# The second tile's normalisation on Pool, and the first transposes copied in another order

## The chip, the cores and the metric

The kernel runs on one core of a Trainium2 chip. The metric is the device time of one execution in microseconds (us). Its engines are TensorE (PE in the profile, with its weight loads as PEld), VectorE (DVE), ScalarE (ACT), Pool (GpSimd) and SyncE (SP), which here only issues transfers. Each engine runs its own instructions in their written order and waits on semaphores for the others.

## The reference

A layer norm without weights feeds two branches, and both are added to x: sliding-window attention (16 heads of 28, window 256) and a gated FFN.

```python
def reference(A_x, A_wqkv, A_wo, B_x, B_w_gate, B_w_up, B_w_down):   # S 2048, D 448, F 1792, bf16
    x = A_x
    xn = (x - mean(x)) / sqrt(var(x) + 1e-5)
    q, k, v = (xn @ A_wqkv) split into 16 heads of 28
    scores = q k^T * 28**-0.5, kept where 0 <= i - j < 256
    attn = softmax(scores) v, heads joined, @ A_wo
    ffn = (gelu(xn @ B_w_gate) * (xn @ B_w_up)) @ B_w_down
    return x + attn + ffn
```

## The kernel before

The 2048 rows of x are 16 tiles of 128 rows (t = 0 to 15), and four blocks of 512 rows (qb = 0 to 3). The body is scheduled by hand: the order in which the instructions are written is the order in which each engine gets them, and semaphores that the framework adds hold an engine until what it reads is there.

Each block needs the normalised x transposed: `xnT` holds the 448 features on partitions, in chunks of 128, and the rows along the free dimension. For one tile of the first block this is made in steps:

- `stat(t)` (L155, L156) on VectorE: the mean and variance of each row.
- `rstd(t, n)` (L160, L161) on ScalarE: Ln and Exp, which give one over the standard deviation.
- `norm(t)` (L170) on VectorE: subtract the mean, multiply by that, 448 elements on each of 128 partitions, into a tile `xn` in bf16. Four buffers of `xn` exist.
- `transp(t, copy, tag)` (L185, L186): four transposes on TensorE into a PSUM bank, and a copy of 512 elements a partition out of it into `xnT`. The bank is given by the tag, "b2" or "b3", and each tag has one buffer; so the transposes of tile 2 wait for the copy of tile 0, and those of tile 3 for the copy of tile 1.

The later tiles are transposed by DMA (`dma_transp`, L176). Behind the first four tiles TensorE does the V products of tiles 0 and 1 (`v_dense`, L190), then the q and k products of the first head group over all four tiles (`proj`, L190). They need all of `xnT` of the first block. From then on, scores (L684), their exponentials on ScalarE (L688), the products with V (L656) and the FFN (L488, L394) are interleaved by the lists in `plan`.

`warmup(n)` (L150) is n matmuls on zeroes ahead of the first data. `pads` (L743) copies weights of q and k into their padded layout. On Pool stand, before all this, the making of the identity and memsets of `v_sb`; the next work on it is the move of half a chunk of `xnT` (L770), behind all four copies, and then the masks (L117).

The order at the start of the first block, as written:

```python
    norm(0)
    stat(2)
    rstd(2, 1)
    transp(0, nc.scalar.copy, "b2")
    norm(1)
    stat(3)
    rstd(3, 1)
    warmup(1)
    transp(1, nc.scalar.copy, "b3")
```

Of the kernel before, what the change touches and what calls it, by code (L numbers as in the profile page):

```python
# [27 lines left out]
def kernel(  # L28
# [11 lines left out]
    nc = tc.nc  # L40
# [22 lines left out]
    x_sb = const.tile([P, NT, D], bf16, name="x_sb")  # L63
# [79 lines left out]
    mv_all = const.tile([P, NT, 2], f32, name="mv_all")  # L143
# [3 lines left out]
    def warmup(n):  # L147
        wps = phase[0].pool.tile([P, 2, QB], f32, name="wps", tag="s")
        for i in range(n):
            nc.tensor.matmul(wps[:, i % 2, :], lhsT=warm[:, 0:P], rhs=warm[:, 0:QB], start=True, stop=True)  # L150


    def stat(t):
        st = work.tile([P, nc.vector.BN_STATS_DIM], f32, name="st")
        nc.vector.bn_stats(out=st[:, :], in_=x_sb[:, t, :])  # L155
        nc.vector.bn_aggr(out=mv_all[:, t, :], in_=st[:, :])  # L156

    def rstd(t, n):
        lnv = work.tile([P, 4], f32, name="lnv")
        nc.scalar.activation(out=lnv[:, 0:n], in_=mv_all[:, t:t + n, 1], func=ACT.Ln, bias=eps_t[:, 0:1], scale=1.0)  # L160
        nc.scalar.activation(out=rstd_all[:, t:t + n], in_=lnv[:, 0:n], func=ACT.Exp, scale=-0.5)  # L161

    xns = {}

    def norm(t):
        xn = work.tile([P, 4, P], bf16, name="xn", bufs=4)
        xf = xn[:, :, :].rearrange("p a b -> p (a b)")
        both = ((0, D, 0), (D, 64, 384))
        for lo, n, src in both if t > 3 else both[:1]:
            nc.vector.tensor_scalar(out=xf[:, lo:lo + n], in0=x_sb[:, t, src:src + n], scalar1=mv_all[:, t, 0:1],  # L170
                                    scalar2=rstd_all[:, t:t + 1], op0=ALU.subtract, op1=ALU.mult)
        xns[t] = xn

# [4 lines left out]
    def transp(t, copy, tag):  # L178


        tp = psum.tile([P, 8, P], bf16, name="tp", tag=tag, bufs=1)
        xn = xns.pop(t)
        xf = xn[:, :, :].rearrange("p a b -> p (a b)")
        for c, lo in enumerate((0, P, 2 * P, D - P)):
            nc.tensor.transpose(out=tp[:, c, :], in_=xf[:, lo:lo + P], identity=ident[:, :])  # L185
        copy(out=xnT[:, :, t * P:(t + 1) * P], in_=tp[:, 0:4, :])  # L186
# [16 lines left out]
    def take(name, cols=QB, tag=None):  # L203

        tag = tag or spare[0]
        spare.remove(tag)
        ps = psum.tile([P, QB], f32, name=name, tag=tag, bufs=1)[:, 0:cols]  # L210
        held[id(ps)] = tag, ps
        return ps
# [6 lines left out]
    def v_dense(t, pv):  # L219
        mm3(pv, lambda c: xnT[:, c, t * P:(t + 1) * P], lambda c: wv[:, c, :], True, False)  # L220
# [531 lines left out]
    stat(1)  # L752
    rstd(1, 1)
    norm(0)
    stat(2)
    rstd(2, 1)
    transp(0, nc.scalar.copy, "b2")
    norm(1)
    stat(3)
    rstd(3, 1)  # L760
    warmup(1)
    transp(1, nc.scalar.copy, "b3")
    pvs = [take("pv", D)]
    v_dense(0, pvs[0])
    norm(2)
    transp(2, nc.scalar.copy, "b2")
    norm(3)
    pads(nc.vector.tensor_copy, wqp, slice(0, 1))
# [290 lines left out]
```

## Time and profile before

| what | us |
|---|---|
| median of 3 runs | 212.53 (212.52 to 212.82) |
| the profiled execution's own time | 212.69 |
| its span in the profile | 210.8 |
| TensorE busy | 205.1 (97% of the span) |
| VectorE busy | 157.8 (75%) |
| ScalarE busy | 132.0 (63%) |
| Pool busy | 48.4 (23%) |

In the profile's rows, the first number is the start in us from the span's start, the second the duration; then engine, line, operation, what it writes and reads, shape and count. A bracket holds the time that the engine stood idle before, and what ended it. Successive instructions on an engine overlap a little: the next one starts some hundredths to a tenth of a us before the row of the one ahead ends. The ends of TensorE's rows are modelled.

### The profile page before, as it was taken

The page shows a single profiled execution, that of the slowest core. Times are in us where ns is not written, and L with a number is a line of the kernel's source. Part 1 is how long each engine was busy: PE and PEld are TensorE (multiplying, and loading weights), DVE is VectorE, ACT ScalarE, POOL GpSimd, SP SyncE. Part 2 cuts the span into 40 slices and gives each one's busy share as a digit, 9 for nine tenths or more (in the row PEclk, how much of TensorE's full clock was granted, in tenths as well). Part 3 has the DMA queues.
Part 4 walks back from the last instruction along what each step waited for, and adds up shares of the span by engine and source line. Part 5 has one row for each costly group of instructions (what it writes and reads, how often), then busy time and mean ns, then how long its engine had stood idle before and what let it go on. Part 6 is the DMA issues. An engine that isn't in the chain of part 4 may idle for free.

```text
span 210.8 us, 6335 instructions
## 1 busy us (share of the span) xinstructions
PE 205.1 (97%) x2678; PEld 96.5 (46%) x2682; DVE 157.8 (75%) x356; ACT 132.0 (63%) x124; POOL 48.4 (23%) x83
## 2 busy tenths in 40 slices
PE   7899999999999999999999999999999999999994
PEld 2333444444444445444445444544444454544562
DVE  6899998999788985696438897395385699659722
ACT  4699588566777977413778788523587787757000
POOL 5388658451000220040000112013000022005100
PEclk9999999999999999999999999999999999999999
DMA  6999989959411001003421000100100010100011
GB/s 176 275 223 230 107 215 220 218 175 234 110 48 48 22 5 39 7 3 71 75 75 47 25 0 27 23 0 15 32 3 0 5 47 0 48 3 0 22 59 41
DMA packets 24889, 15.67 MB, mean 74 GB/s; under 512 B 9208, under 2 KB 24728, under 8 KB 24856
## 3 DMA queue, kind: packets, MB, share of 16 engines
q1 hardware_dynamic: 23814, 14.87, 31.7%
q8 instruction: 22, 0.36, 0.7%
q10 hardware_dynamic: 1042, 0.34, 0.6%
q14 instruction: 11, 0.09, 0.1%
HBM read 9.26 MB, written 2.41 MB: 55 GB/s over the span
## 4 chain that ended last, share of the span: by engine, by line
PE 94%; DVE 2%; ACT 1%; DMA 1%; issue 1%; DVEq 0%; ACTq 0%
PE po L394 24%; PE gt L488 20%; PE u L488 12%; PE ue L488 8%; PE sc L684 7%; PE pq L333 7%; PE ov L656 5%; PE pv L319 4%; PE pq L190 2%; PE pl L394 2%; DVE st L155 1%; PE po L403 1%; DMA x_sb<-in_A_x_dram 1%; PE pv L190 1%; ACT p_sb L688 1%; PE s L190 1%
## 5 line engine op out<-in xcount | busy, mean ns | idle before, releaser
L688 ACT ACTIVATE p_sb<-sc 128x2048 bf16<-128x2048 f32 x39 | 73.2, 1878 | 20.0 <-PE sc L684 14.0
L528 ACT ACTIVATE p_sb<-gt 128x1024 bf16<-128x1024 f32 x28 | 28.7, 1025 | 33.6 <-PE gt L488 30.7
L623 POOL TENSOR_TENSOR oN<-oc,l 128x512 bf16<-128x512 f32 x16 | 21.9, 1374 | 117.9 <-DVE l L636 117.9
L488 PE MATMUL gt<-xnT,wg 64*128 64x512 bf16 x224 | 45.6, 376 | 0.0
L394 PE MATMUL po<-wd,hT 128*128 128x448 bf16 x210 | 43.3, 353 | 0.0
L488 PE MATMUL gt<-xsw,wg 64*128 64x512 bf16 x168 | 40.7, 376 | 0.0
L536 DVE TENSOR_TENSOR hT<-p_sb,u 128x512 bf16<-128x512 bf16 x34 | 21.9, 677 | 15.9 <-PE u L488 15.7
L604 DVE TENSOR_TENSOR p_sb<-p_sb,masks 128x256 bf16<-128x256 bf16 (+1 forms) x90 | 27.9, 365 | 7.5 <-ACT p_sb L688 7.5
L394 PEld LDWEIGHTS <-hT 128*128 128x128 bf16 x238 | 21.8, 98 | 19.5 <-issue 2.4
L488 PEld LDWEIGHTS <-wg 64*128 64x128 bf16 x392 | 19.0, 94 | 22.5 <-issue 0.2
L488 PEld LDWEIGHTS <-wu 64*128 64x128 bf16 x392 | 18.7, 94 | 22.5 <-issue 0.8
L488 PE MATMUL u<-xnT,wu 64*128 64x512 bf16 x136 | 28.1, 376 | 0.0
L488 PE MATMUL u<-xsw,wu 64*128 64x512 bf16 x102 | 24.7, 376 | 0.0
L488 PE MATMUL ue<-xnT,wu 64*128 64x512 bf16 x88 | 18.0, 377 | 0.0
L684 PE MATMUL sc<-qT,kT 28*64 28x320 bf16 (+7 forms) x648 | 16.4, 261 | 0.1
L488 PE MATMUL ue<-xsw,wu 64*128 64x512 bf16 x66 | 16.4, 377 | 0.0
L614 POOL TENSOR_SCALAR_AFFINE_SELECT p_sb<-p_sb 128x512 bf16<-128x512 bf16 (+1 forms) x21 | 14.2, 703 | 6.0 <-ACT p_sb L688 5.9
L641 DVE TENSOR_TENSOR oc<-oc,ov 128x512 f32<-128x512 f32 x12 | 8.2, 681 | 9.1 <-ACT oc L640 9.0
L684 PEld LDWEIGHTS <-kT 28*64 28x64 bf16 (+1 forms) x648 | 7.5, 102 | 13.3 <-issue 12.0
L382 DVE TENSOR_TENSOR res<-po,x_sb 128x448 bf16<-128x448 f32 x13 | 7.7, 621 | 7.7 <-PE po L403 4.4
L505 DVE CAST hT<-ue 128x512 bf16<-128x512 f32 x17 | 11.0, 678 | 1.3 <-PE ue L488 1.2
L170 DVE TENSOR_SCALAR xn<-x_sb,mv_all,rstd_all 128x448 bf16<-128x448 bf16 (+1 forms) x28 | 11.0, 434 | 0.3 <-ACT rstd_all L161 0.3
(111 smaller groups left out, 281.2 us busy)
## 6 DMA issues: line engine op xcount, KB each, us to landing
out_dram<-res SPq DMA_DIRECT2D x15, 112.0 KB
wd<-in_B_w_down_dram SPq DMA_DIRECT2D x2, 784.0 KB
x_sb<-in_A_x_dram SPq DMA_DIRECT2D x3, 448.0 KB
xsw<-xnT SPq DMA_DIRECT2D x6, 192.0 KB
wu<-in_B_w_up_dram SPq DMA_DIRECT2D x4, 224.0 KB
wg<-in_B_w_gate_dram SPq DMA_DIRECT2D x2, 448.0 KB
wu<-in_B_w_up_dram SPq DMA_DIRECT2D x2, 336.0 KB
wg<-in_B_w_gate_dram SPq DMA_DIRECT2D x2, 336.0 KB
```

The lines of the kernel that those rows point to most:

```text
L170: nc.vector.tensor_scalar(out=xf[:, lo:lo + n], in0=x_sb[:, t, src:src + n], scalar1=mv_all[:, t, 0:1], scalar2=rstd_all[:, t:t + 1], op0= ...
L333: nc.tensor.matmul(ps, lhsT=w.rearrange("p h d -> p (h d)"), rhs=xchunk(qb, hi, c, qb * QB, QB), start=c == 0, stop=c == 6, tile_position= ...
L394: nc.tensor.matmul(po[:, 0:w], lhsT=x[:, k, tt * P:(tt + 1) * P], rhs=wt[:, k, lo:up], start=start and n == 0, stop=stop and n == len(term ...
L488: nc.tensor.matmul(ps, lhsT=w[64 * hi:64 * hi + 64, c, p * P:(p + 1) * P], rhs=xchunk(qb, hi, c, qb * QB, QB), start=c == 0, stop=c == 6, ...
L505: copy(out=hTs[qb][:, p + 7 * i, :], in_=us[i])
L528: nc.scalar.activation(out=ges[p][:, :, :], in_=gt[:, :, :], func=ACT.Gelu_apprx_tanh)
L536: nc.vector.tensor_tensor(out=hT[:, p + 7 * i, :], in0=ge[:, i, :], in1=u, op=ALU.mult)
L604: nc.vector.tensor_tensor(out=reg, in0=reg, in1=m, op=ALU.mult)
L614: nc.gpsimd.affine_select(out=reg, in_=reg, pattern=mid + [[1 if diag else -1, min(w, P)]], compare_op=ALU.is_ge, fill=0.0, base=0 if diag ...
L623: nc.gpsimd.tensor_tensor(out=oN[:, g, :], in0=oc[:, :], in1=inv, op=ALU.mult)
L684: nc.tensor.matmul(ss[k0:k0 + nk, j, col:col + nq], lhsT=kT[r, g, kt * P + k0:kt * P + k0 + nk], rhs=qT[r, g, ring(qb).start + q0:ring(qb) ...
L688: nc.scalar.activation(out=p_sb[:, :, 0:ncol], in_=ss[:, :, 0:ncol], func=ACT.Exp, scale=SCALE)
```

## The change

`norm` takes the engine as an argument, and tile 1 is normalised by Pool. Tile 0's transposes and their copy on ScalarE are written ahead of the statistics of tile 2 (and so of the third Ln/Exp). The statistics of tiles 2 and 3 follow each other on VectorE. Tile 2's normalisation comes directly behind them, ahead of tile 1's transposes, and the copy of those is done by VectorE in place of ScalarE. TensorE's and SyncE's instructions keep their order.

```diff
-    def norm(t):
+    def norm(t, eng=nc.vector):
...
-            nc.vector.tensor_scalar(out=xf[:, lo:lo + n], in0=x_sb[:, t, src:src + n], scalar1=mv_all[:, t, 0:1],
+            eng.tensor_scalar(out=xf[:, lo:lo + n], in0=x_sb[:, t, src:src + n], scalar1=mv_all[:, t, 0:1],
                                     scalar2=rstd_all[:, t:t + 1], op0=ALU.subtract, op1=ALU.mult)
         xns[t] = xn
...
     stat(1)
     rstd(1, 1)
     norm(0)
+    norm(1, nc.gpsimd)
+    transp(0, nc.scalar.copy, "b2")
     stat(2)
     rstd(2, 1)
-    transp(0, nc.scalar.copy, "b2")
-    norm(1)
     stat(3)
     rstd(3, 1)
     warmup(1)
-    transp(1, nc.scalar.copy, "b3")
+    norm(2)
+    transp(1, nc.vector.tensor_copy, "b3")
     pvs = [take("pv", D)]
     v_dense(0, pvs[0])
-    norm(2)
     transp(2, nc.scalar.copy, "b2")
     norm(3)
     pads(nc.vector.tensor_copy, wqp, slice(0, 1))
```

## The prediction

> **What bounds the kernel now.** I read the page first, for its chain of work that ended last, then the busy time by stages, then that chain in order of time over the first 24 us, and last the timeline of each engine around the change.
>
> ```profile
> PE 94%; DVE 2%; ACT 1%; DMA 1%; issue 1%; DVEq 0%; ACTq 0%
> ```
>
> The chain is TensorE for 94% of the span. By stages (the stretch, its length, busy time and instructions of TensorE, its weight loads, VectorE, ScalarE and Pool, then clock, DMA share, GB/s):
>
> ```profile
> 19.50:60.00 40.50, 40.34 (x467) 18.14 (x465) 36.98 (x75) 28.26 (x23) 18.62 (x35) 1.00 0.87 178
> ```
>
> From 19.5 us TensorE is busy 40.34 of 40.50 us, and DMA, busy 0.87 of that stage, does not hold it. So an edit in the first 9 us is worth only what it moves the start of TensorE's unbroken work. The chain says where that start is:
>
> ```profile
> 7.19 0.48 ACT xnT L186
> ...
> 7.72 0.38 PE tp L185 x4
> 8.10 0.57 PE pv L190 x3
> 8.67 1.42 PE s L190 x6
> ```
>
> The fourth transposes (at 7.72) are released by the end of ScalarE's copy of the second tile's transposes (7.19 to 7.67), which frees the bank "b3". Behind them come the second V product and, at 8.67 in the chain, the first q and k products. The engines' own rows (start, duration, what; in brackets the idle time before) show how tight that meeting is. VectorE:
>
> ```profile
> 5.41 0.18 DVE L156 BATCH_NORM_AGGREGATE mv_all<-st 128x2 f32<-128x6 f32 x1
> 5.51 0.37 DVE L170 TENSOR_SCALAR xn<-x_sb,mv_all,rstd_all 128x448 bf16<-128x448 bf16 x1
> 5.79 0.62 DVE L155 BATCH_NORM_STATS2 st<-x_sb 128x6 f32<-128x448 bf16 x1
> 6.45 0.18 DVE L156 BATCH_NORM_AGGREGATE mv_all<-st 128x2 f32<-128x6 f32 x1
> 6.55 0.37 DVE L170 TENSOR_SCALAR xn<-x_sb,mv_all,rstd_all 128x448 bf16<-128x448 bf16 x1
> 7.23 0.40 DVE L170 TENSOR_SCALAR xn<-x_sb,mv_all,rstd_all 128x448 bf16<-128x448 bf16 x1 [0.32 <-ACT rstd_all L161]
> 7.54 0.27 DVE L743 COPY wqp<-wraw 128x336 bf16<-128x336 bf16 x1
> 8.14 0.42 DVE L186 COPY xnT<-tp 128x512 bf16<-128x512 bf16 x1 [0.33 <-PE tp L185]
> 8.48 0.27 DVE L781 COPY w3p<-wraw 128x448 bf16<-128x448 bf16 x1
> ```
>
> ScalarE:
>
> ```profile
> 4.81 0.20 ACT L161 ACTIVATE rstd_all<-lnv 128x1 f32<-128x1 f32 x1
> 5.63 0.29 ACT L160 ACTIVATE lnv<-mv_all,eps_t 128x1 f32<-128x1 f32 x1 [0.62 <-DVE mv_all L156]
> 5.96 0.20 ACT L161 ACTIVATE rstd_all<-lnv 128x1 f32<-128x1 f32 x1
> 6.06 0.57 ACT L186 COPY xnT<-tp 128x512 bf16<-128x512 bf16 x1
> 6.67 0.29 ACT L160 ACTIVATE lnv<-mv_all,eps_t 128x1 f32<-128x1 f32 x1
> 6.99 0.20 ACT L161 ACTIVATE rstd_all<-lnv 128x1 f32<-128x1 f32 x1
> 7.10 1.17 ACT L186 COPY xnT<-tp 128x512 bf16<-128x512 bf16 x2
> ```
>
> TensorE:
>
> ```profile
> 4.85 0.39 PE L185 MATMUL tp<-ident,xn 128*128 128x128 bf16 x4
> 5.07 0.38 PE L150 MATMUL wps<-wo 128*128 128x512 bf16 x1
> 5.93 0.40 PE L185 MATMUL tp<-ident,xn 128*128 128x128 bf16 x4 [0.48 <-DVE xn L170]
> 6.69 0.74 PE L190 MATMUL pv<-wv,xnT 128*128 128x448 bf16 x3 [0.36 <-ACT xnT L186]
> 7.26 0.84 PE L185 MATMUL tp<-ident,xn 128*128 128x128 bf16 x8
> 7.94 0.73 PE L190 MATMUL pv<-wv,xnT 128*128 128x448 bf16 x3
> 8.62 0.82 PE L190 MATMUL s<-xnT,wqp 128*128 128x512 bf16 x3
> ```
>
> Tiles are called 0 to 3. The rows at 5.51, 6.55 and 7.23 are the normalisations of tiles 1, 2 and 3; those at 5.79 and 6.45 the statistics of tile 3. On ScalarE 5.63/5.96 and 6.67/6.99 are Ln/Exp of tiles 2 and 3; between them, at 6.06, stands the copy of tile 0's transposes, and 7.10 holds the copies of tiles 1 and 2. On TensorE 4.85 and 5.93 are the transposes of tiles 0 and 1, and 7.26 those of 2 and 3. Tile 3's transposes wait for two things that end almost together: its normalisation, 7.23 + 0.40 = 7.63, and the free bank, 7.67. VectorE's copy (8.14 + 0.42 = 8.56) then releases the q product at 8.62. To gain, both gates must come earlier.
>
> **The change part by part.** All in the profiled execution's time, whose span is 210.8 us inside 212.69 us.
>
> *Second normalisation off VectorE.* It held VectorE from 5.51 to the next instruction at 5.79, 0.28 us. Tile 3's statistics now start at 5.51 in place of 5.79, their aggregate follows 0.66 later (5.79 to 6.45 in the rows), at 6.17, and ends 0.18 later, at 6.35 in place of 6.63.
>
> *Tile 0's copy ahead of the third Ln/Exp.* The transposes end at 4.85 + 0.39 = 5.24; a copy started 0.04 after such an end (8.14 against 8.10). So it runs 5.28 to 5.85 where it ran 6.06 to 6.63. Ln of tile 2 had its data by 5.59 and starts at about 5.80, not 5.63; Exp 0.33 behind it, at 6.13, ends at 6.33 in place of 6.16. Ln of tile 3 starts at 6.39 (0.04 after 6.35), Exp ends 0.52 later, at 6.91 in place of 7.19. That is the first gain, 0.28 us.
>
> *VectorE's tail.* Tile 2's normalisation waits for 6.33, starts at 6.36 (before: 6.55) and lets the next instruction start 0.28 later, at 6.64. There now stands the copy of tile 1's transposes, moved here from ScalarE. By the row at 8.14 it takes 0.42 us and lets the next start after 0.34: it runs 6.64 to 7.06, and tile 3's normalisation starts at 6.98, within 0.03 of when its Exp lets it (6.95), against 7.23. It ends at 7.38 and the bank is free at 7.06. The gates 7.63 and 7.67 become 7.38 and 7.06: tile 3's transposes go from 7.72 to about 7.43, its copy from 8.14 to 7.87, the q product from 8.62 to 8.35. Gain 0.27 us. What is late next is VectorE itself, full from 5.51 to 7.6, and Exp of tile 3, 0.03 behind it.
>
> *TensorE and ScalarE beside that.* TensorE's order is unchanged. The first V product waited for the copy that ended at 6.63; now that ends at 5.85 and the product fits between tile 1's transposes and tile 2's, which can start at 6.36 + 0.37 + 0.05 = 6.78. If its weights land late it cannot start after 6.69, where it ran before; then tiles 2 and 3 follow from 7.26 and 7.48, which costs 0.05 us. ScalarE copies tile 2 from about 7.2 to 7.8, before tile 3's copy is done. All this costs nothing, under the cover of VectorE's tail.
>
> *The normalisation on Pool: the unknown.* No row shows a tensor_scalar on Pool. Pool waits there for Exp of tile 1 (4.81 + 0.20 = 5.01) and starts at about 5.08, 0.07 behind (the rows above show 0.04 between VectorE and ScalarE; the rest is allowance). Queued behind it on Pool is only the move of half a chunk (L770), which starts at 8.74 and for which Pool stood idle 5.1 us; so no other work waits for it.
>
> ```profile
> L623 POOL TENSOR_TENSOR oN<-oc,l 128x512 bf16<-128x512 f32 x16 | 21.9, 1374 | 117.9 <-DVE l L636 117.9
> L614 POOL TENSOR_SCALAR_AFFINE_SELECT p_sb<-p_sb 128x512 bf16<-128x512 bf16 x18 | 11.0, 637 | 4.3 <-ACT p_sb L688 4.3
> ...
> L614 POOL TENSOR_SCALAR_AFFINE_SELECT p_sb<-p_sb 128x1024 bf16<-128x1024 bf16 x3 | 3.3, 1099 | 1.7 <-ACT p_sb L688 1.6
> ...
> L770 POOL COPY xnT<-xnT 64x512 bf16<-64x512 bf16 x1 | 0.6, 607 | 5.1 <-ACT wkp L743 5.1
> ```
>
> With one input, affine selects go from 637 ns at 512 elements to 1099 at 1024: 0.90 ns an element on 0.17 us, so 0.58 us for 448. L770's copy, 607 ns for 512, gives 0.55. With two fp32 inputs, 1374 ns for 512 gives about 1.22. This one has one bf16 input and two scalars for each partition, so it is nearest to the one-input rows; I take 0.65 us, bounds 0.55 to 1.22. Nothing lets it be below the plain copy. With 0.65 Pool ends at 5.73, tile 1's transposes run about 5.78 to 6.18, and VectorE's copy at 6.64 finds them done. That copy is held only when Pool ends after 6.64 - 0.44 = 6.20, which is a duration over 1.12 us. From there each microsecond on Pool is one of delay: the transposes 0.05 and 0.40 behind it, 0.04 to the copy, 0.34 to tile 3's normalisation, so that starts at 5.08 + X + 0.83 for a duration X, and equals the old 7.23 at X = 1.32. At the bound of 1.22 the gain is still 0.10. In the Trainium skill, "GPSIMD Engine Reference", section "Elementwise — side-by-side cycle accounting", gives 2.6 cycles an element at 1.2 GHz where VectorE takes 1; as an estimate that is 0.97 us for 448 elements, and by it the sum would be the same 0.27, with 0.15 us left of the cover. No run here shows that figure for this operation.
>
> The other question is whether Pool and VectorE hinder each other. They can:
>
> ```profile
> 17.50 0.64 DVE L170 TENSOR_SCALAR xn<-x_sb,mv_all,rstd_all 128x448 bf16<-128x448 bf16 x1
> ```
> ```profile
> 16.77 1.23 POOL L614 TENSOR_SCALAR_AFFINE_SELECT p_sb<-p_sb 128x512 bf16<-128x512 bf16 x2
> ```
>
> This normalisation of 448 elements takes 0.64 us, where the quiet ones above take 0.37 to 0.40; it ends at 18.14, just behind Pool's selects (16.77 + 1.23 = 18.00). What runs on VectorE from 5.08 to 6.35 after the change are statistics, and these are not slowed beside Pool:
>
> ```profile
> 14.50 0.62 DVE L155 BATCH_NORM_STATS2 st<-x_sb 128x6 f32<-128x448 bf16 x1
> ```
> ```profile
> 14.53 3.47 POOL L614 TENSOR_SCALAR_AFFINE_SELECT p_sb<-p_sb 128x1024 bf16<-128x1024 bf16 x5
> ```
>
> 0.62 us against 0.62 to 0.63 elsewhere. So I put contention at nothing, as long as Pool is done by 6.36, a duration under 1.28 us. The Trainium skill, "SBUF — State Buffer", section "SBUF: two separate sides", says that a VectorE operation that uses two ports and a Pool operation share one port pair, and whichever starts first keeps it for its whole instruction. By that rule, with which both rows agree, tile 2's normalisation would wait for Pool's end if Pool ran past 6.36.
>
> *Sum.* 8.62 to 8.35, -0.27 us, bounds -0.28 (Exp of tile 3 alone) and -0.10 (the two-input price). I take -0.26. The profiled execution would go from 212.69 to 212.43; the median of the runs is 212.53 (212.52 to 212.82), so its like would be 212.27.
>
> **The rivals.** *The normalisation on Pool is slow.* If the two scalars for each partition make it dearer than any row of Pool shows for such a size, everything hangs on Pool: tile 2's normalisation is held to its end too, and TensorE's in-order queue holds the first V product behind tile 1's transposes. By the formula it turns to a loss at 1.32 us; at 2.0 us the loss is 0.68, so 213.2; a loss over 0.43 us needs 1.75 us, 1.3 times the dearest Pool row of 512 elements. Against it: one input, not two, and bf16. For it: no row shows the form. I give 0.20 to 1.75 us and beyond, and 0.08 to the stretch between 1.22 and 1.75, whose time is 212.4 to 213.0.
>
> *The shift is swallowed.* The first products come 0.27 earlier and then meet something that did not move: a weight transfer still under way, or SyncE, which sends its transfers one behind the other whatever the engines do. Then the time is 212.5. For it: DMA is busy 0.87 from 19.5 to 60 us. Against it: in that stage TensorE idles only 0.16 us in all, and transfers have 1% of the chain, so each later one had some slack. I give 0.12.
>
> *More comes out of it than the sum.* The work behind 8.67 has other orders that 0.27 us might undo a wait in, and runs of one kernel lie 0.30 apart. The q and k stage would have to give another 0.17 us to reach 212.1, as its rows show no such reserve in TensorE's 40.34 of 40.50. I give 0.17 to a time of 212.0 to 212.1.
>
> **How the numbers follow.** Forecast 0.43, with 212.27; more 0.17; swallowed 0.12; Pool between 0.08; Pool slow 0.20. What a measurement of this kernel can tell from no change is about 0.2%, here 0.43 us: 212.10 to 212.96. Faster by more: 0.17. Slower by more: 0.20. Within: 0.43 + 0.12 + 0.08 = 0.63. The range goes from 212.05, which takes in most of the case of more, to 212.85, a Pool duration of 1.64 us; it leaves out the slow Pool and little else. Within it the forecast's own runs from 212.25 to 212.45.
>
> **What would show it.** In the profile after: the Pool row of the normalisation starts near 5.08 and takes 0.55 to 1.22 us; the copy of tile 0 on ScalarE stands at 5.28, Exp of tile 3 ends at 6.91, VectorE's copy of tile 1 starts at 6.64, the last normalisation at 6.98, the q product at 8.35, and and the first exponential of scores 0.27 us earlier than before. A Pool row over 1.32 us would make the forecast wrong at its unknown; a q product at 8.35 with an unchanged end would make it wrong behind that; statistics over 0.63 us beside Pool would make the price of contention wrong.

## The result, and the profile after

The changed kernel takes 213.26 us in the median of 20 runs (213.12 to 214.69), the kernel before 212.70 us in 20 runs beside it (212.51 to 213.12). The ratio of the runs is 1.0041, 95% interval 1.0032 to 1.0050: slower, by more than the 0.2% that can be told from no change. The medians lie 0.56 us apart (0.26%); the ratio is larger because four of the 20 runs lie at 214.5 to 214.7, of which more below. The profiled execution takes 213.26 us, beside 212.69 before.

The chain of work that ended last, in order of time (start, duration, what):

```profile
4.81 0.21 ACT rstd_all L161
5.02 0.10 issue
5.12 1.87 POOL xn L170
6.99 0.05 issue
7.04 0.40 PE tp L185 x4
7.43 0.57 PE pv L190 x3
8.00 0.24 PE tp L185 x4
8.24 0.02 issue
8.26 0.40 PE tp L185 x4
8.65 0.57 PE pv L190 x3
9.22 1.42 PE s L190 x6
```

In the chain before, VectorE and then ScalarE led from the statistics to tile 3's transposes. Now the chain leaves VectorE after the second statistics, goes through Ln and Exp of tile 1 to Pool, stays there for 1.87 us, and runs on TensorE without a gap worth naming. The q product (9.22 here) stood at 8.67. The engines' rows, VectorE, ScalarE and TensorE:

```profile
5.43 0.59 DVE L155 BATCH_NORM_STATS2 st<-x_sb 128x6 f32<-128x448 bf16 x1
6.06 0.18 DVE L156 BATCH_NORM_AGGREGATE mv_all<-st 128x2 f32<-128x6 f32 x1
6.93 0.40 DVE L170 TENSOR_SCALAR xn<-x_sb,mv_all,rstd_all 128x448 bf16<-128x448 bf16 x1 [0.70 <-ACT rstd_all L161]
7.47 0.42 DVE L186 COPY xnT<-tp 128x512 bf16<-128x512 bf16 x1
7.81 0.39 DVE L170 TENSOR_SCALAR xn<-x_sb,mv_all,rstd_all 128x448 bf16<-128x448 bf16 x1
```

```profile
5.88 0.59 ACT L186 COPY xnT<-tp 128x512 bf16<-128x512 bf16 x1 [0.87 <-PE tp L185]
6.37 0.30 ACT L160 ACTIVATE lnv<-mv_all,eps_t 128x1 f32<-128x1 f32 x1
6.70 0.20 ACT L161 ACTIVATE rstd_all<-lnv 128x1 f32<-128x1 f32 x1
6.81 0.28 ACT L160 ACTIVATE lnv<-mv_all,eps_t 128x1 f32<-128x1 f32 x1
7.12 0.20 ACT L161 ACTIVATE rstd_all<-lnv 128x1 f32<-128x1 f32 x1
```

```profile
5.21 0.63 PE L185 MATMUL tp<-ident,xn 128*128 128x128 bf16 x4
5.64 0.63 PE L150 MATMUL wps<-wo 128*128 128x512 bf16 x1
7.04 0.40 PE L185 MATMUL tp<-ident,xn 128*128 128x128 bf16 x4 [0.76 <-POOL xn L170]
7.27 0.73 PE L190 MATMUL pv<-wv,xnT 128*128 128x448 bf16 x3
7.84 0.82 PE L185 MATMUL tp<-ident,xn 128*128 128x128 bf16 x8
8.49 0.73 PE L190 MATMUL pv<-wv,xnT 128*128 128x448 bf16 x3
9.17 0.82 PE L190 MATMUL s<-xnT,wqp 128*128 128x512 bf16 x3
```

VectorE's statistics of tile 3 end at 6.24 (6.06 + 0.18; before 6.63), 0.11 us earlier than the 6.35 of the forecast. Then VectorE idles 0.70 us until Exp of tile 2. On ScalarE tile 0's copy starts at 5.88, since tile 0's transposes ran 5.21 to 5.84 in place of 4.85 to 5.24, and both Ln/Exp pairs queue behind it. The copy of tile 1, on VectorE at 7.47, waits for tile 1's transposes (7.04), and those for Pool. From there everything is late by one amount: the q product 9.17 against 8.62. The stage in which TensorE is never idle is as it was:

```profile
19.50:60.00 40.50, 40.50 (x473) 18.08 (x470) 37.30 (x75) 28.16 (x24) 19.13 (x35) 1.00 0.82 173
```

40.50 of 40.50 us busy. So the whole loss arises before 9.2 us: 0.55 us at the q product, 0.57 us in the execution's own time.

### The profile page after: what moved, and what is told of

It reads as the page before. It is cut to its first block, busy times and chain, and to the rows that moved or that the text cites. A ratio compares the mean times of both kernels' runs of the same rounds, so it can differ in the third digit from the quotient of the medians.

```text
span 211.4 us, 6341 instructions
## 1 busy us (share of the span) xinstructions
PE 206.2 (98%) x2682; PEld 96.9 (46%) x2682; DVE 158.0 (75%) x356; ACT 131.4 (62%) x123; POOL 50.3 (24%) x84
## 4 chain that ended last, share of the span: by engine, by line
PE 94%; ACT 1%; DMA 1%; DVE 1%; POOL 1%; issue 0%; DVEq 0%; ACTq 0%
PE po L394 24%; PE gt L488 20%; PE u L488 12%; PE ue L488 8%; PE sc L684 7%; PE pq L333 7%; PE ov L656 5%; PE pv L319 4%; PE pq L190 2%; PE pl L394 2%; PE pv L190 1%; PE po L403 1%; DMA x_sb<-in_A_x_dram 1%; ACT p_sb L688 1%; POOL xn L170 1%; PE s L190 1%
## 5 line engine op out<-in xcount | busy, mean ns | idle before, releaser
L604 DVE TENSOR_TENSOR p_sb<-p_sb,masks 128x256 bf16<-128x256 bf16 (+1 forms) x90 | 27.9, 365 | 7.5 <-ACT p_sb L688 7.5
```

The source lines that it names most:

```text
L604: nc.vector.tensor_tensor(out=reg, in0=reg, in1=m, op=ALU.mult)
```

## The experiments

Two theories at the start: **P**, the loss is the duration of Pool's instruction; **C**, it is ScalarE's new order, in which tile 0's copy, late when TensorE's clock rises late, holds the third and fourth Ln/Exp. A third, **W**, is about the runs near 214.6: in them TensorE's clock rose late, because TensorE waited; its rival **D** has the first transfers land late instead. Ratios are to the kernel before on the same chip, with their 95% interval.

**Pool alone**, run in two batches.

```diff
-    norm(1)
+    norm(1, nc.gpsimd)          # in its old place; nothing else changed
```

> The kernel before with one part of the change: tile 1 normalised by Pool, in its old place; order and copies as before. Theory P (the loss is Pool's own duration, 1.86 us): Pool 5.12 to 6.98, tile 1's transposes near 7.03, ScalarE's copy of them near 7.45 to 8.02, tile 3's transposes wait for that bank, near 8.07 in place of 7.72, so +0.35 us, about 213.05 beside 212.7. By the shared port pair VectorE's normalisation of tile 2, ready near 6.16, is held to about 7.1. Theory C (the loss comes from ScalarE's new order, tile 0's copy ahead of the third Ln/Exp, when TensorE's transposes are late): no part of that order is here, so 212.7.

213.06 us against 212.63, ratio 1.0020 (1.0010 to 1.0029); the second batch 213.06 against 212.57. As P says, and C, which has no part in this kernel, cannot say: one moved instruction costs 0.43 us. The part of the expectation on the shared port pair failed; its rows are in the last section.

**All but Pool.**

```diff
-    norm(1, nc.gpsimd)
     transp(0, nc.scalar.copy, "b2")
     stat(2)
     rstd(2, 1)
+    norm(1)
     stat(3)
```

> The change without its Pool part: tile 1 is normalised by VectorE behind the third statistics, as before; tile 0's copy ahead of the third Ln/Exp and tile 1's copy on VectorE are kept. Theory P: no loss, tile 3's transposes gated by its normalisation at about 7.63, 212.6 to 212.7. Theory C: ScalarE's third and fourth Ln/Exp stay late (Exp of tile 3 ends near 7.3, not 7.19), +0.15 to +0.4 us, 212.85 to 213.1.

212.90 us, ratio 1.0007 (0.9998 to 1.0016), runs from 212.48 to 213.58. Its profile is of the longest run. ScalarE's rows there (tile 0's copy and Exp of tile 3), and then VectorE's:

```profile
5.90 0.59 ACT L186 COPY xnT<-tp 128x512 bf16<-128x512 bf16 x1 [0.90 <-PE tp L185]
7.13 0.20 ACT L161 ACTIVATE rstd_all<-lnv 128x1 f32<-128x1 f32 x1
```

```profile
6.95 0.40 DVE L170 TENSOR_SCALAR xn<-x_sb,mv_all,rstd_all 128x448 bf16<-128x448 bf16 x1 [0.39 <-ACT rstd_all L161]
7.26 0.42 DVE L186 COPY xnT<-tp 128x512 bf16<-128x512 bf16 x1
7.59 0.39 DVE L170 TENSOR_SCALAR xn<-x_sb,mv_all,rstd_all 128x448 bf16<-128x448 bf16 x1
```

Here tile 0's transposes also ran slowly (5.23 to 5.86), the copy starts at 5.90, Exp of tile 3 ends at 7.33, and on VectorE tile 2's normalisation, tile 1's copy and tile 3's normalisation follow without a gap, so the last starts at 7.59 in place of 7.23, and the q product at 8.96 in place of 8.62. This delay of 0.34 us has no Pool in it: it is C's, with tile 1's copy standing between the two normalisations. It is not the whole of the 213.58, because a transfer was late behind it:

```profile
13.04 0.33 DVE L743 COPY wkp<-wraw 128x336 bf16<-128x336 bf16 x1 [0.82 <-DMA wraw<-in_A_wqkv_dram]
```

In the profile of before this copy stood at 11.79 and waited for nothing. The scores that stood at 16.54 come at 17.56, 1.02 us later, so about two thirds of this execution's loss is the transfer's. The version with half on Pool, below, shows C without that. In other executions there is no loss: the lowest run is 212.48.

**Tile 0's copy ahead, alone**, and **tile 1's copy on VectorE, alone**.

```diff
+    transp(0, nc.scalar.copy, "b2")      # first kernel
     stat(2)
     rstd(2, 1)
-    transp(0, nc.scalar.copy, "b2")
```
```diff
+    norm(2)                              # second kernel
-    transp(1, nc.scalar.copy, "b3")
+    transp(1, nc.vector.tensor_copy, "b3")
```

> The kernel before with one part of the change: tile 0's transposes and their copy on ScalarE are written ahead of the third Ln/Exp. Everything else as before. Theory C (a late clock of TensorE makes tile 0's copy start at 5.9 and, first in ScalarE's order, hold the third and fourth Ln/Exp): in executions with the late clock Exp of tile 3 ends near 7.3 in place of 7.19 and tile 1's copy, behind it, near 7.8, so +0.15 us; with the early clock 0. Median 212.65 to 212.85. If the order costs nothing: 212.63 with the spread of the kernel before.

212.77 us, ratio 1.0004 (0.9995 to 1.0013): no difference that can be told. Its profile, of the lowest run, has tile 0's transposes at 0.47 us, so it says nothing of an execution in which they take 0.63.

> The kernel before with one part of the change: tile 1's transposes are copied by VectorE, behind tile 2's normalisation, in place of ScalarE. VectorE was idle 0.32 us there: copy near 6.83 to 7.25, tile 3's normalisation near 7.23 as before. Expected 0 to -0.05 us, 212.6. If the copy holds tile 3's normalisation: up to +0.34, 212.9.

212.62 us, ratio 0.9999 (0.9986 to 1.0012). In its profile the q product comes 0.09 us earlier (8.53), and yet that execution took 212.95, because of this row on VectorE (the second fence has it as it was before):

```profile
9.39 0.63 DVE L155 BATCH_NORM_STATS2 st<-x_sb 128x6 f32<-128x448 bf16 x1 [0.72 <-DMA x_sb<-in_A_x_dram]
```
```profile
8.69 0.63 DVE L155 BATCH_NORM_STATS2 st<-x_sb 128x6 f32<-128x448 bf16 x1
```

The statistics of tile 4 waited for x until 9.39, and the copy of k, which the first scores need, is queued behind them; the first exponential of scores starts at 12.10 in place of 11.73. An earlier start can thus be swallowed by a transfer, as one of the rivals had it.

**The price on Pool.** Two theories: **S**, the price goes with the size; **F**, most of it is paid once, by the first instruction of the form. The kernel before, with ten extra Pool instructions in the third block.

```diff
+            for _ in range(2):       # scr is a free xn buffer, its content unused
+                nc.gpsimd.tensor_scalar(out=scr[:, 0:D], in0=x_sb[:, 1, :], scalar1=mv_all[:, 1, 0:1], scalar2=rstd_all[:, 1:2], ...)
+                ...                  # 224 elements; one scalar; two constants; a copy
```

> The kernel before with extra Pool instructions in the third block, their result unused, each run twice: tensor_scalar with two scalars for each partition on 448 and on 224 elements, with one such scalar on 448, with two constants on 448, and a copy of 448. Theory F: the first tensor_scalar takes about 1.9 us, the second of the same size 0.55 to 0.7. Theory S: both of 448 take about 1.86, that of 224 about 1.0; the copy takes 0.55 in both.

Pool's rows, the first of all and the second pass:

```profile
127.89 2.39 POOL L882 TENSOR_SCALAR xn<-x_sb,mv_all,rstd_all 128x448 bf16<-128x448 bf16 x1
...
135.66 1.86 POOL L882 TENSOR_SCALAR xn<-x_sb,mv_all,rstd_all 128x448 bf16<-128x448 bf16 x1
137.62 1.11 POOL L883 TENSOR_SCALAR xn<-x_sb,mv_all,rstd_all 128x224 bf16<-128x224 bf16 x1
138.83 1.41 POOL L884 TENSOR_SCALAR xn<-x_sb,rstd_all 128x448 bf16<-128x448 bf16 x1
140.32 1.72 POOL L885 TENSOR_SCALAR xn<-x_sb 128x448 bf16<-128x448 bf16 x1
142.10 0.56 POOL L886 COPY xn<-x_sb 128x448 bf16<-128x448 bf16 x1
```

Two scalars for each partition: 1.86 us for 448 elements, 1.11 for 224, which is 3.3 ns an element on 0.36 us. One such scalar 1.41, two constants 1.72, a copy 0.56. Theory S stands. In the first pass the two took 2.39 and 1.24 (130.38). Beside both, VectorE multiplied exponentials by masks (L604, 0.82 us at 127.88 and at 129.82), which it did not do beside the second pass; that this held Pool was not tried.

**A small instruction of the same form ahead of it.**

```diff
     nc.vector.memset(eps_t[:, :], 1e-5)
+    nc.gpsimd.tensor_scalar(out=pre[:, :], in0=ident[:, 0:4], scalar1=eps_t[:, 0:1], scalar2=eps_t[:, 0:1], ...)
```

> The changed kernel with one more Pool instruction: a tensor_scalar of the same form, but 4 elements, while Pool is idle between the memsets (end 3.66) and tile 1's normalisation (5.12). Theory F (most of the 1.86 us is paid once, by the first tensor_scalar on Pool): the small one takes about 1.2 us and the normalisation 0.55 to 0.7; tile 1's transposes are then no longer late. Where TensorE's clock has risen by tile 0's transposes, the q product comes near 8.35 and the time is about 212.4; where it has not, tile 0's copy at 5.9 holds Ln/Exp and the time is about 212.9, as without Pool. Theory S (1.86 us is the size's price, 4 ns an element): the small one takes 0.2 us, the normalisation 1.86, the time stays at 213.25.

> As the version before, and tile 0's transposes and their copy are moved back behind the third Ln/Exp (the order of the kernel before), so that a late clock of TensorE cannot hold the third Ln/Exp. Theory F with theory C: Exp of tile 2 ends near 6.1 and tile 0's copy 6.1 to 6.7 whatever the clock, Exp of tile 3 near 7.1, its normalisation 7.15 to 7.55, the q product near 8.5: -0.1 us, 212.5 to 212.6, with little spread. Theory S: Pool ends at 6.98 as before and the loss of about 0.5 us stays, 213.2.

213.38 and 213.25 us, ratios 1.0060 (1.0038 to 1.0081) and 1.0034 (1.0021 to 1.0047). Pool's rows of the second:

```profile
3.58 0.38 POOL L122 TENSOR_SCALAR pre<-ident,eps_t 128x4 bf16<-128x4 bf16 x1
5.20 1.87 POOL L170 TENSOR_SCALAR xn<-x_sb,mv_all,rstd_all 128x448 bf16<-128x448 bf16 x1 [1.24 <-ACT rstd_all L161]
```

0.38 us for four elements, 1.87 for 448: nothing is paid once. Theory F is gone. Four of the first version's ten runs are of the kind near 214.6; its others lie at 213.17 to 213.41. So with Pool unchanged the order on ScalarE made no difference that shows.

**Half of it on Pool.**

```diff
-    norm(1, nc.gpsimd)
+    norm(1, nc.gpsimd, 0)                # columns 0 to 223
...
+    norm(1, part=1)                      # columns 224 to 447, VectorE, behind stat(3)
     norm(2)
```

> The changed kernel with a smaller dose on Pool: Pool normalises columns 0 to 223 of tile 1, VectorE columns 224 to 447 behind the statistics of tile 3. By the measured Pool price (1.11 us for 224 elements with two scalars) Pool ends near 6.23 in place of 6.98, tile 1's transposes come near 6.5. Theory P (Pool's duration is the loss): the loss falls to what the version without Pool has, median 212.5 to 212.9. If the loss is a matter of Pool being used at all or of ScalarE's order: 213.2.

212.97 us, ratio 1.0010 (0.9999 to 1.0022).

```profile
5.16 1.12 POOL L170 TENSOR_SCALAR xn<-x_sb,mv_all,rstd_all 128x224 bf16<-128x224 bf16 x1 [1.51 <-ACT rstd_all L161]
```

Pool's time falls by 0.74 us, and the loss from 0.55 to 0.30, the level of the version without Pool (0.27), with the q product at 8.94 and 8.96 in the two profiles. Pool is no longer in the chain of this profile, whose execution took 212.91. The chain goes from tile 0's transposes to their copy on ScalarE (5.89), Exp of tile 2 (6.70), VectorE's copy (7.25) and tile 3's normalisation to the q product, 0.32 us late: that is C, with tile 1's copy again between the two normalisations. A dose that ends by 6.28 no longer shows a cost of its own.

**A version without Pool that should gain.**

```diff
-    norm(1, nc.gpsimd)
     transp(0, nc.scalar.copy, "b2")
...
     warmup(1)
-    norm(2)
-    transp(1, nc.vector.tensor_copy, "b3")
+    norm(1)
     pvs = [take("pv", D)]
     v_dense(0, pvs[0])
+    transp(1, nc.scalar.copy, "b3")
+    norm(2)
...
-    transp(3, nc.vector.tensor_copy, "b3")
+    transp(3, nc.vector.tensor_copy, "b1")   # and the V products of tiles 1 and 3 into b3 and b1
```

> A version without Pool: tile 1 is normalised by VectorE behind the statistics of tile 3; tile 0's copy is ahead of the third Ln/Exp; the first V product goes ahead of tile 1's transposes; tile 1's copy stays on ScalarE, and tile 3's transposes use bank b1 (the second V product b3), so that they do not wait for tile 1's copy. If the start of the first q product sets the time: Exp of tile 3 near 6.91, its normalisation at 6.95 to 7.35, its transposes near 7.40, the q product near 8.33 in place of 8.62, -0.25 us, about 212.45. If TensorE's clock rises late in the run, tile 0's copy is late, Exp of tile 3 ends near 7.3 and the gain is gone (212.7).

212.98 us, ratio 1.0004 (0.9990 to 1.0018): no gain. Its profiled execution, one of 214.53, shows the first V product on TensorE:

```profile
7.15 1.28 PE L190 MATMUL pv<-wv,xnT 128*128 128x448 bf16 x3 [0.86 <-DMA wv<-in_A_wqkv_dram]
```

It waited 0.86 us for the weights of v, in TensorE's order ahead of three tiles' transposes, and then took 1.28 us in place of 0.73. The statistics of tile 2 had waited for x too, 0.73 us, until 5.55. What held the other runs is not shown. No tried version beats the kernel before.

**The runs near 214.6.** The changed kernel was run again, with a profile each:

> The changed kernel as it is, on the same chip as the two others: +0.55 us beside before in the median, and some runs in five at 214.5 to 214.7. Its profile shows either kind.

213.22 us against 212.67, ratio 1.0029 (1.0011 to 1.0047), three of 12 runs at 214.58 to 214.67, the profile being of one. TensorE's rows there:

```profile
7.08 0.61 PE L185 MATMUL tp<-ident,xn 128*128 128x128 bf16 x4 [0.80 <-POOL xn L170]
7.48 1.33 PE L190 MATMUL pv<-wv,xnT 128*128 128x448 bf16 x3
8.60 1.06 PE L185 MATMUL tp<-ident,xn 128*128 128x128 bf16 x8
9.45 1.32 PE L190 MATMUL pv<-wv,xnT 128*128 128x448 bf16 x3
10.57 0.85 PE L190 MATMUL s<-xnT,wqp 128*128 128x512 bf16 x3
```

> The changed kernel once more, for one profile. If it is one of the runs at 214.5 to 214.7: theory W says that TensorE's products between 7 and 9.4 us take twice the usual time (a clock that rises late); theory D says that the first rows of x or the weights of v land about 1.3 us later than usual.

This one took 213.19 and shows the common kind. In the late one transfers were in time (the first statistics start at 2.91), but transposes take 0.61 in place of 0.40 and V products 1.33 in place of 0.73 until the q product at 10.57: theory W's prediction for the profile, not D's. Then the gap in front of tile 1's transposes was filled, and widened:

```diff
-    warmup(1)
+    warmup(3)          # after_warm3, twice; after_warm0: the line removed
```

> The changed kernel with three warm-up matmuls in place of one between the transposes of tiles 0 and 1, while TensorE would wait for Pool (0.76 us idle there). Theory W: the changed kernel's runs at 214.5 to 214.7 (4 of 20) are those in which TensorE's clock rose late because TensorE was idle while it waited for Pool; then those runs go, and the median stays at 213.25. Rival: those runs have another cause and stay at about one in five.

> The changed kernel with three warm-up matmuls in place of one, once more. In 42 runs of the changed kernel and its version with one more Pool instruction 12 lay at 214.5 to 214.9; with three warm-ups 0 of 10. A profile of such a run has TensorE's clock low until 10.6 us. Theory W (TensorE's idle 0.8 us before tile 1's transposes leaves the clock low for one more period): again none, or one in twelve at most. Rival (chance): about three in twelve.

> The changed kernel without the warm-up matmul between the transposes of tiles 0 and 1: TensorE is idle 0.4 us longer there. Theory W: more runs at 214.5 to 214.9 than three in twelve. Rival: as many or fewer.

> The kernel before with tile 1 normalised by Pool, once more: TensorE idles there as long as in the changed kernel, but 0 of 11 runs were late. Theory W says that some runs must be late here too, about three in twelve; if again none is, idle time alone is not the cause.

Three warm-ups: medians 213.24 and 213.26, so the loss of the median is no matter of this kind; none of 16 runs over 214.3, and one at 214.04 had its first x tile 0.89 us late (3.77 in place of 2.88). No warm-up: 213.28, 3 of 10 at 214.3 to 214.8. Pool alone: 0 of 11, then 2 of 11, the profile of one with the first V product at 1.33 us too. The changed kernel as it is: 7 of 33 (the expectations count one more, 12 where it is 11 of 42); with the small Pool instruction 4 of 10 and 0 of 6. The version without Pool in which TensorE waited 0.86 us for weights: 1 of 12, the one in the profile above. The four versions whose profiles have no wait over 0.62 us there (all but Pool, each of the copies alone, half on Pool): 0 of 46. The kernel before: in 104 runs beside these one at 214.10, the others under 213.6.

So the late clock goes with TensorE waiting some 0.8 us or more until about 7.1 us, with Pool or without. That matmuls in that gap take it away is likely but not shown: were the seven late runs spread by chance over the 49 with one and with three warm-ups, none would fall on the 16 with three in about 5% of cases. Why Pool alone had fewer is open.

## Why the prediction was wrong

**The step that failed is the price of Pool's instruction.** I took 0.65 us within 0.55 to 1.22, from the rows of copies and selects, and as the upper end a product of two fp32 inputs. It measures 1.86. A tensor_scalar with two operations and two scalars for each partition costs 3.3 ns an element where a select costs 0.90 and the two-input product about 2.3; the rows that I called nearest were near in their operands but not in what Pool does with them, and the top of the bounds was the dearest row that happened to be there, with no reason why nothing is dearer. Why this form is so dear stays open: with one scalar for each partition it took 1.41, with two constants 1.72. The Trainium skill, "GPSIMD Engine Reference", section "Elementwise — side-by-side cycle accounting", has its 2.6 cycles an element from a two-input add; the estimate of 0.97 us that the prediction worked out from them was half of what was measured.

**The formula around it held.** Tile 3's normalisation at Pool's start + X + 0.83: 5.12 + 1.86 + 0.83 = 7.81, and it stands at 7.81. The rival "the normalisation on Pool is slow" gave a loss of X - 1.32, 0.54 us; the q product moved by 0.55 and the profiled execution by 0.57. Its threshold for a measurable loss, 1.75 us, was passed. It had a chance of 0.20 and the range ended below it.

**Tile 0's copy at 5.28 was wrong too.** I read the moment at which tile 0's transposes end, 5.24, off one execution, in which TensorE ran fast by 4.85. In 11 of the 15 profiles of the experiments those transposes take 0.61 to 0.63 us, ending near 5.84 in all but one of them. In the old order that cost nothing, since ScalarE copied tile 0 at 6.06 at the earliest; in the new one it moves Exp of tile 3 from the 6.91 of the forecast to 7.32, later than the 7.19 before. The cover that I named for it, "VectorE's tail", was thinner than I said: without Pool the change is no gain but somewhere between 0 and 0.3 us of loss, by medians. The two losses do not add: tile 1's copy waits for Pool or for tile 2's normalisation, whichever is later.

**The weights of v** could land later than 6.69: they held the first V product to 6.90 in one profile (tile 0's copy ahead, alone), to 7.15 in another, and to 7.75 in the version with tile 0's copy moved back. "It cannot start after 6.69" was one execution's luck.

**What was right:** that the start of TensorE's unbroken work counts (in the profile of after by itself; in two others a late transfer behind or ahead of the first scores added its own delay); the step from one VectorE instruction to the next (copy at 7.47, normalisation at 7.81, 0.34); that the statistics are not slowed by Pool (0.59 us beside it); that an earlier start can be swallowed by a transfer, which the case with tile 1's copy alone showed.

## What to carry to other kernels

An instruction moved to an engine on which its form has not been seen has no upper bound from other forms; measure it there first, in a stretch of the same kernel in which that engine is idle, which costs one run. Put the break-even duration beside the price: here a duration over 1.32 us was a loss, and the fact that the gain could never exceed 0.28 us while the loss had no bound should have moved the chances. In the first microseconds of a kernel, read the times of TensorE and of transfers from several executions before an in-order engine is made to wait for them.

## What the runs showed of the hardware

**TensorE's clock at the start.** Matmuls on zeroes run 0.43 us apart at first (their weight loads in the profile of before, at 2.24, 2.67 and 3.10), and the rise comes at another moment in each execution. It is over by 4.85 us in the profile of before, where tile 0's transposes take 0.39 us. It lies between 6 and 7 in that of after (0.63 for tile 0's, 0.40 for tile 1's at 7.04), and near 10.5 in the late one, behind the second V product of 1.32. The granted clock does not show it: for the stretch with V products of 1.33 us the table by stages says 1.00 (the third number from the end).

```profile
7.00:8.50 1.50, 1.42 (x7) 0.86 (x8) 1.11 (x4) 0.29 (x2) 0.02 (x1) 1.00 1.03 324
```

The Trainium skill, "TensorE: Matmul & The Clock Gate", section "Part 1: The HAM clock gate (the "warmup" mystery)", has a free-running window of about 3.4 us in which TensorE must be busy before its clock doubles, so that the count of slow matmuls varies with the run. The traces agree in kind: the common and the late rise are some 3.5 to 4.5 us apart, an idle 0.8 us goes with the late one, and no run here shows the window itself.

**Pool and VectorE beside each other.** The rows of the prediction showed a normalisation on VectorE held to the end of Pool's selects. Beside Pool's tensor_scalar it depends on when it starts. In Pool alone (VectorE, then Pool):

```profile
6.20 0.37 DVE L170 TENSOR_SCALAR xn<-x_sb,mv_all,rstd_all 128x448 bf16<-128x448 bf16 x1
```

```profile
5.19 1.86 POOL L170 TENSOR_SCALAR xn<-x_sb,mv_all,rstd_all 128x448 bf16<-128x448 bf16 x1 [1.55 <-ACT rstd_all L161]
```

it runs at 0.37 us in the middle of Pool's 1.86. In the version with tile 0's copy moved back, the same normalisation starts 0.43 us ahead of Pool's end (5.20 + 1.87 = 7.07) and lasts until 7.20:

```profile
6.64 0.56 DVE L170 TENSOR_SCALAR xn<-x_sb,mv_all,rstd_all 128x448 bf16<-128x448 bf16 x1
```

With three warm-ups one that starts 0.50 us ahead of Pool's end (7.37; 6.01 + 1.86 = 7.87) takes 0.63, until 8.00. The second batch of Pool alone has one that starts 0.82 us ahead of it and takes 0.36. The rule by which the prediction and the expectation reckoned, that whoever starts first keeps the ports for its whole instruction, would have held that one and the one at 6.20 too; for these two instructions beside each other the rows decide against it. Pool seems to hold what VectorE needs in the last part of its instruction only; why was not tried.
